# Scores of two tiles in one go, and a new order of loads, in a fused attention and feed-forward kernel

## The chip, the cores and the metric

The kernel runs on one core of one Trainium2 chip. The metric is device time in microseconds (us) from launch to end, as the median of several runs. Engines are named as in the profile: PE (TensorE, matrix products), DVE (VectorE), ACT (ScalarE), POOL (GpSimd) and SP (SyncE); PEld is PE's loading of weights.

## The reference, cut to what matters

Attention by chunks of 32 queries over 4 batches, 8 heads, 768 positions and head size 64, and then a gated feed-forward layer.

```
for c in range(24):                                   # chunks of 32 queries
    k_full = concat(mem_k, k[c*32-16 : c*32+32+8])     # 8 memory rows, 16 left, 32 own, 8 right
    scores = q_c @ k_full.T / 8
    a = exp(scores - max(scores)); a = a / sum(a)
    out[c] = a @ concat(mem_v, v[same rows])
x = out as [3072, 512]
y = (relu(x @ w_gate) * (x @ w_val)) @ w_out          # d_ff = 1536
```

Inputs are float32; the kernel casts on loading and computes in 16 bits with float32 sums.

## The kernel before, in words

A **tile** is 128 positions of one batch with all 8 heads: 24 tiles, a = 0 to 23, six per batch. Each goes through these steps, each an `op` of the plan (key in brackets):

- q and k are transposed (`t`) and copied into qT and kT (`tc`, `kc`). Tiles 0 to 5 come as pairs by `load_pair`; from tile 14 (q) or 15 (k) on the transposes are DMAs of SP's queue, before that PE products.
- `scores` (`s`, L289): 32 products of 64 rows x 32 columns of weights, moving 64 columns each, into the one buffer s_ps ([128, 2, 512] float32, pool `sps` with one buffer). A tile uses 256 of the 512 columns of each half.
- Row maximum (`max`), subtraction (`sub`), row sum (`sum`), reciprocal and normalisation (`nrm`) on DVE, the exponential (`exp`) on ACT. `sub` gives s_ps back.
- The probabilities are transposed (`p`, L348, by DMA from tile 14 on), copied (`pc`), multiplied with v_bd (`values`, `v`, L365), and the product is copied into xT (`x`).

v_bd holds v block by block with the memory rows: two sets, batch b in set b % 2. Set 0 is first filled with a pattern from mem_v (`pattern_load` on ACT's queue, cast, eight `spread` copies); then `load_v_rows` (L188) writes rows of v over it. The first chunk of the first batch has no left context, so `v_parts` gives it a small load of its own. Rows of batch b >= 2 can be loaded only when `values` of the last tile of batch b - 2 are done: the load of batch 2 depends on tile 5 and that of batch 3 on tile 11.

The **feed-forward part** works on blocks of tiles (`BLOCKS`, 3 or 4 tiles). `first` (`f`, L411) makes g_ps and v_ps for one of 12 slices m of d_ff; ACT does the relu, DVE the product (L423). `second` (`o`, L432) multiplies with w_out. Weights come in groups, w0 to w4 (slices 0-1, 2-3, 4-5, 6-8, 9-11). The two blocks of the first batch run their slices group by group in turn; the later blocks run one after the other. xT has two buffers, and a block gives its buffer back with its last `f`. Until the first block can start, PE is kept busy with `idle_product` (L403).

All loads with a cast are issued by POOL in the order of `LOADS`: Kr and Qr are pairs, `i` makes the identity matrix, vxy are v rows of batch 0 (half x, head pair y), w, o (w_out in halves), m (memory rows for later batches), z (zeroing of set 1), kN and qN single tiles, bxy v rows of batch x, head pair y (two loads each).

**The order of every engine's work** is worked out before by `schedule()`: it walks through time with a cost for each op, gives each engine the ready op of lowest priority value, and writes the ops down in that order. `LEAD` shifts the earliest start of later blocks' attention (`pace`), the priorities of the spreads and other small things. A load may be issued when fewer than 8 loads are in flight (`flying`); its data counts as there 1.5, 2.4 or 4.0 us after its turn on the queue ends. On the chip each engine follows the written order and waits by semaphores.

Of the kernel before, what the change touches and what calls it, by code (L numbers as in the profile page):

```python
# [10 lines left out]
F32 = mybir.dt.float32  # L11
# [10 lines left out]
def kernel(  # L22
# [27 lines left out]
    KW = CH + NMEM  # L50
    CTX = 16 + CH + 8
    NSET = 2
    BLOCKS = [3, 3, 3, 4, 3, 4, 4]
    LEAD = [22, -5, 16, 12, 4, 3, 14, 23, 5, -6, 7, 17, 24, 4, 24, 12, 12, 0, 3, -6, -3]
    LAST = ((0, 384), (384, 512))
    BY_DMA = (14, 15)
    BY_DMA_P = 14
    LANDING = 3.0
    PAIRS = 3
    SPLIT = 1  # L60
    EARLY = 2
    MEM_BY_SP = 0
    MEM_LEAD = (0,0,4,4)
    BY_DMA_X = 24
    BESIDE = 10.0
    LOADS = """K0 Q0 K1 i v01 Q1 Q2 K2 v00 v02 v03 w0 v12 w1 z1 v13 v11 w2 v10 w3
               m z3 w4 q7 q6 q8 z0 k8 k6 q9 k7 o1 k23 k9 o0 k13 z2 b13 b12 q13
               q21 k16 q12 b11 b10 k10 q17 k20 k11 q10 k18 q16 b21 q11 k15 q18 q14 k12 k14 b23
               b22 k21 k22 q15 b20 b30 q19 q20 q23 q22 b32 k17 b33 b31 k19"""

    KEY_RUNS = ((CH, KW, 0), (0, CH, NMEM), (KW, 64, KW))
    assert sum(BLOCKS) == NT and NMEM == 8 and D == 64 and H == 8
# [115 lines left out]
    def load_v_rows(b, par, hp, s0, s1, c0, c1):  # L188
# [2 lines left out]
            bass.AP(tensor=v.tensor, offset=v[b, 2 * hp + par, 0, 0].offset + (CH * c0 + s0 - 16) * D,  # L191
                    ap=[[D, s1 - s0], [CH * D, c1 - c0], [1, D]]))

    def v_parts(b, par, hp, c0, c1):
        parts = []
        if (b, par, hp, c0) == (0, 0, 0, 0):
            parts.append((b, par, hp, 16, CTX, 0, 1))
            c0 = 1
        if (b, par, hp, c1) == (B - 1, 1, HP - 1, NCH):
            c1 -= 1  # L200
            parts.append((b, par, hp, 0, 48, c1, c1 + 1))
        return parts + [(b, par, hp, 0, CTX, c0, c1)]
# [85 lines left out]

    def scores(a):  # L289
        b, t = divmod(a, TPB)  # L290
        s = sps.tile([128, 2, 512], F32, name="s_ps")
        keys = kT[b].rearrange("p h c s -> p h (c s)")
        for h2 in range(HP):
            for g in range(4):
                c = 4 * t + g
                lo, hi = max(KW * c - 16, 0), min(KW * c + 48, NCH * KW)
                o0 = 64 * h2 + lo - (KW * c - 16)
                for r in range(2):
                    d = slice(D * r, D * r + D)
                    nc.tensor.matmul(s[CH * g:CH * g + CH, r, o0:o0 + hi - lo],  # L300
                                     lhsT=qT[b][d, h2, CH * c:CH * c + CH],
                                     rhs=keys[d, h2, lo:hi], start=True, stop=True)
        S_ps[a] = s.rearrange("p a (h s) -> p a h s", s=64)[:, :, 0:HP, :]

    def row_max(a):
        t = a % TPB
# [154 lines left out]
    def psum(n):  # L461
# [3 lines left out]
    MARGIN = 1.2  # L465


    op("warm", {"DVE": 0.15}, lambda e: nc.vector.memset(warm, 0.0), prio=(-9,))
    op("warm2", {"ACT": 1.5}, lambda e: nc.scalar.activation(warm, warm, ACT.Exp), ["warm"], prio=(-9,), after=["vml"])  # L469
    op("vm00", {"DVE": 0.3}, lambda e: nc.vector.memset(vmem_0.rearrange("p h d -> p (h d)").bitcast(F32), 0.0),  # L470
       prio=(-8,), after=["im"])
    op("vml", {"ACT": 0.7}, lambda e: pattern_load(), prio=(-10,))
    op("kml", {"SP": 1.3}, lambda e: mem_load(), prio=(-8,))
    op("im", {"DVE": 0.12}, lambda e: nc.vector.memset(ident_h.bitcast(F32), 0.0), prio=(-8.5,), after=["warm"])
    op("ib", {"DVE": 0.25}, lambda e: nc.vector.tensor_copy(ident_b, ident_h), ["ident"], prio=(-7,))
# [45 lines left out]
    for a in range(NT):  # L521
        b, t = divmod(a, TPB)
        last = t == TPB - 1
        for i in (1, 0):
            if a < 2 * PAIRS:
                if a % 2:
                    continue
                ps = "fps" if a // 2 < EARLY else "aps"
                op(("t", a, i), {"PE": 0.64}, lambda e, a=a, i=i: pair_t(a // 2, i), [("qk2", a // 2, i), "ib", ("kv", b)],
                   (1, a - i, 0), [ps], ["pr"], pace(max(a - i, 0)))  # L530
                if i:
                    parts = k_parts(a // 2)
                    for n, (j, c0, c1) in enumerate(parts):
                        d = 0.07 + 0.0713 * (c1 - c0)
                        op(("kc", a // 2, n), {"ACT": d, "DVE": d},
                           lambda e, a=a, j=j, c0=c0, c1=c1: pair_k_copy(a // 2, j, c0, c1, engine[e]),
                           [("kc", a // 2, n - 1) if n else ("t", a, i)], (1, a - i + n // 2, n % 2), (),
                           [ps] * (n == len(parts) - 1))
                else:
                    for x in range(2):  # L540
                        op(("tc", a + x, i), {"ACT": 0.64, "DVE": 0.65}, lambda e, a=a, x=x: pair_q_copy(a // 2, x, engine[e]),
                           [("tc", a, i) if x else ("t", a, i)], (1, a + x, 0), (), [ps] * x)
            elif a < BY_DMA[i]:
                op(("t", a, i), {"PE": 0.23}, lambda e, a=a, i=i: qk_t(a, i), [("qk", a, i), "ib", ("kv", b)],
                   (1, a - i, 0), ["aps"], ["qk"], pace(max(a - i, 0)))
                op(("tc", a, i), psum(HP * 128), lambda e, a=a, i=i: qk_copy(a, i, engine[e]), [("t", a, i)],
                   (1, a - i, 0), (), ["aps"])
            else:
                op(("t", a, i), {"SP": 1.3}, lambda e, a=a, i=i: qk_dma(a, i), [("qk", a, i), ("kv", b)],
                   (1, a - i, 0), ["kt"] * i, ["qk"], [("p", a - i - 4)])  # L550
                if i:
                    op(("tc", a, i), {"ACT": 0.5}, lambda e, a=a, i=i: qk_copy(a, i, engine[e]),
                       [("t", a, i)], (1, a - i, 0), (), ["kt"], [("s", a - 2)] + pace(a - 1))
                else:
                    op(("tc", a, i), {"PE": 0.01}, lambda e: None, [("t", a, i)], (1, a - i, 0))
        op(("s", a), {"PE": 0.36}, lambda e, a=a: scores(a),
           [("tc", a, 0), keys_of(a), ("new", b) if b else ("new", 0, t // 3)] + ([] if last else [keys_of(a + 1, True)]),
           (1, a, 1), ["sps"],
           ["kv"] if last else [], ([("s", a - 1)] if a else []) + (pace(a) if a >= BY_DMA[0] else []) + behind(a))
# [14 lines left out]
        blk = block_of[a]  # L574
        j = a - starts[blk]
        ready = [("vl", b, 0 if b else t // 3, n) for n in range(2 * HP)]
        ready += [("mr", b, par, hp) for par in range(2) for hp in range(HP)] if b else []
        if a < BY_DMA_X:
            op(("v", a), {"PE": 0.41}, lambda e, a=a: values(a), [("pc", a)] + ready, (1, a, 10),
# [124 lines left out]
    def schedule():  # L704
# [30 lines left out]
        while len(started) < len(ops) + len(loads):  # L735
# [8 lines left out]
            while moved:  # L744
                moved = False
                for e in ("POOL", "PE", "ACT", "DVE", "SP"):
                    if free[e] > t + 1e-9:
                        continue
                    if e == "POOL":
# [97 lines left out]
```

## Time and profile before

| what | value |
|---|---|
| median of 3 runs | 239.06 us (238.92 to 239.76) |
| the profiled execution's own time | 238.81 us |
| its span, first to last instruction | 237.0 us |
| PE busy | 225.5 us (95%) |
| DVE busy | 150.9 us (64%) |
| ACT busy | 117.8 us (50%) |
| POOL busy | 91.5 us (39%) |
| granted TensorE clock | 1.000 |

The profile page tells busy time by engine, then by 40 slices of the span, then the chain of work that ended last, then groups of instructions. The timeline is a list of merged instructions with start and length. Products on PE overlap one another, so a group's length runs past the start of the next; what a group costs PE is read from start to start.

### The profile page before, as it was taken

Reading aid. Unit: us, or ns where it says so; the run is one execution under the profiler, and the core shown is the slowest. Engines: PE = TensorE matmul, PEld = TensorE weight load, DVE = VectorE, ACT = ScalarE, POOL = GpSimd, SP = SyncE. Lnnn points to the kernel's source line nnn. Section 1 sums busy time; section 2 is a strip of 40 time slices with the busy share of each in tenths; the row PEclk is TensorE's granted clock in tenths of the full one; section 3 lists DMA queues with packets and bytes.
Section 4 is the critical chain, followed back from the end, with each engine's and each line's share of the span. In section 5 each row is a group of like instructions: output and inputs, shape, how many; then the busy total and the mean of one; then the engine's idle time right before and its main releaser. Section 6 shows DMA issues by size and latency. Waiting matters only on the chain.

```text
span 237.0 us, 5892 instructions
## 1 busy us (share of the span) xinstructions
PE 225.5 (95%) x2432; PEld 125.6 (53%) x2432; DVE 150.9 (64%) x267; ACT 117.8 (50%) x251; POOL 91.5 (39%) x107
## 2 busy tenths in 40 slices
PE   0988989999999999999999999999999999999994
PEld 0777655665544666655444545664454444444442
DVE  5789953468999789954999146797775520234300
ACT  7988735444442786653643356655553331333212
POOL 6989998884875787059430000000000000000000
PEclk9999999999999999999999999999999999999999
DMA  7999999999999999979999344545420002200022
GB/s 75 163 160 179 161 180 179 165 192 172 151 174 211 199 179 133 118 127 149 141 150 117 75 149 111 69 46 121 127 48 0 0 4 88 88 0 0 3 88 89
DMA packets 121147, 27.17 MB, mean 115 GB/s; under 512 B 111264, under 2 KB 118176, under 8 KB 121120
## 3 DMA queue, kind: packets, MB, share of 16 engines
q0 software_dynamic: 101376, 16.61, 94.7%
q1 hardware_dynamic: 19664, 10.16, 18.5%
q8 instruction: 19, 0.31, 0.6%
q14 instruction: 8, 0.07, 0.1%
q10 hardware_dynamic: 80, 0.02, 0.0%
HBM read 33.24 MB, written 6.29 MB: 167 GB/s over the span
## 4 chain that ended last, share of the span: by engine, by line
PE 84%; POOL 8%; DMA 3%; ACT 2%; issue 1%; ACTq 0%; POOLq 0%
PE out_ps L432 26%; PE v_ps L411 25%; PE g_ps L411 25%; POOL v_bd L189 5%; PE xT_ps L365 4%; DMA v_bd<-in_v_dram 3%; PE s_ps L300 2%; PE qk_ps L266 2%; POOL w_gate_sb L121 1%; POOL w_val_sb L121 1%; POOL qk_p L220 1%; PE pT_ps L348 1%; ACT v_bd L94 1%; POOL v_bd L135 1%; ACT L469 1%
## 5 line engine op out<-in xcount | busy, mean ns | idle before, releaser
L423 DVE TENSOR_TENSOR gvT<-v_ps,g_relu 128x384 f16<-128x384 f32 (+1 forms) x84 | 51.2, 610 | 42.4 <-PE v_ps L411 42.0
L411 PE MATMUL v_ps<-xT,w_val_sb 128*128 128x384 f16 (+1 forms) x336 | 75.9, 349 | 0.3 <-DMA w_val_sb<-in_moe_w_val_dram 0.3
L411 PE MATMUL g_ps<-xT,w_gate_sb 128*128 128x384 f16 (+1 forms) x336 | 75.9, 349 | 0.0
L417 ACT ACTIVATE g_relu<-g_ps 128x384 f16<-128x384 f32 (+1 forms) x84 | 44.8, 534 | 57.9 <-PE g_ps L411 47.4
L432 PE MATMUL out_ps<-w_out_sb,gvT 128*128 128x512 f16 (+2 forms) x300 | 65.5, 370 | 0.0
L411 PEld LDWEIGHTS <-w_gate_sb 128*128 128x128 f16 x336 | 32.1, 98 | 28.1 <-DMA w_gate_sb<-in_moe_w_gate_dram 0.4
L411 PEld LDWEIGHTS <-w_val_sb 128*128 128x128 f16 x336 | 31.3, 98 | 26.8 <-DMA w_val_sb<-in_moe_w_val_dram 0.5
L189 POOL DMA_DIRECT2D v_bd<-in_v_dram x42 | 37.7, 910 | 16.6 <-PE xT_ps L365 9.3
L432 PEld LDWEIGHTS <-gvT 128*128 128x128 f16 x300 | 28.0, 98 | 30.0
L94 ACT COPY o_sb<-out_ps 128x512 f32<-128x512 f32 (+2 forms) x25 | 14.2, 569 | 32.8 <-PE out_ps L432 32.4
L164 DVE TENSOR_TENSOR v_bd<-vmem 8x768 int32<-8x768 int32 (+1 forms) x29 | 26.6, 944 | 1.1 <-ACT vmem L94 0.9
L327 ACT ACTIVATE p_exp<-dif 128x64 f16<-128x64 f32 (+2 forms) x72 | 19.6, 336 | 8.9 <-DVE dif L320 8.7
L313 DVE TENSOR_REDUCE mx<-s_ps 128x8 f32<-128x512 f32 x24 | 16.3, 677 | 5.5 <-PE s_ps L300 5.2
L331 DVE TENSOR_REDUCE sm<-p_exp 128x8 f32<-128x512 f16 x24 | 16.3, 678 | 5.2 <-ACT p_exp L327 5.1
L211 POOL DMA_DIRECT2D qk_b<-in_k_dram x18 | 16.0, 891 | 5.5 <-DMA w_out_sb<-in_moe_w_out_dram 2.8
L211 POOL DMA_DIRECT2D qk_b<-in_q_dram x18 | 16.0, 902 | 5.0 <-DMA v_bd<-in_v_dram 1.6
L342 DVE TENSOR_TENSOR p_n<-p_exp,rinv 128x512 f16<-128x512 f16 x24 | 16.4, 684 | 0.3
L320 DVE TENSOR_TENSOR dif<-s_ps,mx 128x512 f32<-128x512 f32 x24 | 16.4, 682 | 0.1
L365 PEld LDWEIGHTS <-v_bd 128*128 128x128 f16 x384 | 12.7, 96 | 5.2 <-issue 1.3
L365 PE MATMUL xT_ps<-pT,v_bd 128*128 128x32 f16 x384 | 13.0, 176 | 0.9 <-DMA v_bd<-in_v_dram 0.7
L94 ACT CAST xT<-xT_ps 128x512 f16<-128x512 f32 x17 | 9.9, 587 | 7.3 <-PE xT_ps L365 7.0
L403 PE MATMUL idle_ps<-ident_h 128*128 128x128 f16 x87 | 8.4, 238 | 4.8 <-POOL ident_h masks.py:199 4.8
(46 smaller groups left out, 125.5 us busy)
## 6 DMA issues: line engine op xcount, KB each, us to landing
out_dram<-o_sb SPq DMA_DIRECT2D x23, 256.0 KB, 2.1
v_bd<-in_v_dram POOLq DMA_DIRECT2D x23, 168.0 KB, 9.6
qk_b<-in_q_dram POOLq DMA_DIRECT2D x18, 128.0 KB, 9.3
qk_b<-in_k_dram POOLq DMA_DIRECT2D x18, 128.0 KB, 9.2
w_out_sb<-in_moe_w_out_dram POOLq DMA_DIRECT2D x2, 768.0 KB, 10.8
v_bd<-in_v_dram POOLq DMA_DIRECT2D x15, 84.0 KB, 4.9
qk_p<-in_k_dram POOLq DMA_DIRECT2D x3, 256.0 KB, 5.9
qk_p<-in_q_dram POOLq DMA_DIRECT2D x3, 256.0 KB, 5.3
```

Of the source, the lines that this page charges most:

```text
L94: nc.scalar.copy(o, i)
L164: nc.vector.tensor_tensor(out=o, in0=i, in1=i, op=ALU.bitwise_or)
L189: nc.gpsimd.dma_start(v_bd[b % NSET][64 * par + NMEM + s0:64 * par + NMEM + s1, hp, c0:c1, D * par:D * par + D], bass.AP(tensor=v.tensor, ...
L211: nc.gpsimd.dma_start(qk_b[a, i], bass.AP(tensor=x.tensor, offset=x[b, 0, 128 * t, 0].offset, ap=[[D, 128], [S * D, H], [1, D]]))
L320: nc.vector.tensor_tensor(out=SM[a, "dif"].rearrange("p h r s -> p r h s"), in0=S_ps.pop(a), in1=mx_b, op=ALU.subtract)
L327: nc.scalar.activation(p[:, :, :, s0:s0 + k1 - k0], dif[:, :, :, k0:k1], ACT.Exp, scale=SCALE)
L342: nc.vector.tensor_tensor(out=P_n[a], in0=SM.pop((a, "p")), in1=rinv_b, op=ALU.mult)
L365: nc.tensor.matmul(ps[:, hp, r], lhsT=v_bd[b % NSET][:, hp, 4 * t + g, :], rhs=x[:, hp, r], start=True, stop=True)
L411: nc.tensor.matmul(ps, lhsT=w[:, f, 128 * m:128 * m + 128], rhs=xTs[blk][:, f, :], start=(f == 0), stop=(f == NFC - 1))
L417: nc.scalar.activation(st["r", m], st.pop((0, m)), ACT.Relu)
L423: nc.vector.tensor_tensor(out=st["gv"][:, m, :], in0=st.pop((1, m)), in1=st.pop(("r", m)), op=ALU.mult)
L432: nc.tensor.matmul(st["o", t, cols], lhsT=st["gv"][:, m, 128 * t:128 * t + 128], rhs=w_out_sb[:, m, slice(*cols)], start=(m == 0), stop=(m ...
```

## The change

Four things: (1) from tile 6 on, the scores of tiles a and a+1 (a even) are one step of PE, side by side in the two 256-column parts of s_ps, and the buffer is given back after the second subtraction; (2) v rows of the first chunk are loaded by SP as float32 into vmem_f, behind a memset that clears 32 rows of it, and copied into v_bd by ACT or DVE; the pattern's load on ACT's queue now waits for that memset; (3) the plan counts a load as in flight until 0.2 us after its data is there, not until 1.0 us after its turn; (4) LOADS, LEAD and BLOCKS are new, so the blocks cut the tiles otherwise: 3, 3, 4, 4, 2, 4, 4.

```
-    BLOCKS = [3, 3, 3, 4, 3, 4, 4]
-    LEAD = [22, -5, 16, 12, 4, 3, 14, 23, 5, -6, 7, 17, 24, 4, 24, 12, 12, 0, 3, -6, -3]
+    BLOCKS = [3, 3, 4, 4, 2, 4, 4]
+    LEAD = [0, 1, 19, 16, 6, 23, 13, -1, -4, 7, 17, -5, 13, -6, 0, 6, 12, 4, -6, 3, -6]
+    TWO = 6
-    LOADS = """K0 Q0 K1 i v01 Q1 Q2 K2 v00 v02 v03 w0 v12 w1 z1 v13 v11 w2 v10 w3
-               m z3 w4 q7 q6 q8 z0 k8 k6 q9 k7 o1 k23 k9 o0 k13 z2 b13 b12 q13
-               q21 k16 q12 b11 b10 k10 q17 k20 k11 q10 k18 q16 b21 q11 k15 q18 q14 k12 k14 b23
-               b22 k21 k22 q15 b20 b30 q19 q20 q23 q22 b32 k17 b33 b31 k19"""
+    LOADS = """K0 Q0 i K1 Q1 v03 Q2 K2 v02 v00 v01 w0 v13 w1 w2 v10 v11 v12 w3 q7
+               q6 q10 k8 o0 z1 k7 k10 q9 m k6 w4 k9 q8 k13 o1 z0 b11 k11 z3 k21
+               k20 k12 z2 b12 b13 q21 b10 k15 q11 k18 q13 b22 k16 k23 k14 q15 b20 q14 q23 q22
+               q18 q12 b33 q16 q17 b21 b23 b31 k17 k19 k22 b30 q20 q19 b32"""
...
+    def load_first():
+        nc.sync.dma_start(vmem_f[NMEM + 16:64, 0, 0:D], ... v[0, 0, 0, 0] ... [[D, 64 - NMEM - 16], [1, D]])
...
     def v_parts(b, par, hp, c0, c1):
         if (b, par, hp, c0) == (0, 0, 0, 0):
-            parts.append((b, par, hp, 16, CTX, 0, 1))
             c0 = 1
...
     def scores(a):
-        s = sps.tile([128, 2, 512], F32, name="s_ps")
+        if a >= TWO and a % 2:
+            s = TMP.pop(("s", a - 1))
+        else:
+            s = TMP["s", a] = sps.tile([128, 2, 512], F32, name="s_ps")
+        h0 = HP * (a >= TWO and a % 2)
...
+    op("vf0", {"DVE": 0.1}, ... memset(vmem_f[0:32, 0, 0:D], 0.0), prio=(-10,))
+    op("vfl", {"SP": 0.4}, lambda e: load_first(), ["vf0"], prio=(-7.5,), after=["kml"])
+    op("vfc", {"ACT": 0.15, "DVE": 0.15}, ... copy(v_bd[0][0:64, 0, 0, 0:D], vmem_f[0:64, 0, 0:D]),
+       [("vfl", 3.2), ("vml", 1.2), ("spread", 0, 0)], prio=(1, 0, 9))
-    op("vml", {"ACT": 0.7}, lambda e: pattern_load(), prio=(-10,))
+    op("vml", {"ACT": 0.7}, lambda e: pattern_load(), ["vf0"], prio=(-10,))
...
-                       ... [("s", a - 2)] + pace(a - 1))     # k copy behind a DMA transpose
+                       ... [("s", a - 4)] + pace(a - 2))
...
+        if a >= TWO and a % 2:
+            op(("s", a), {"PE": 0.01}, lambda e: None, [("s", a - 1)], ...)
+        elif a >= TWO:
+            op(("s", a), {"PE": 0.60}, lambda e, a=a: (scores(a), scores(a + 1)), score_deps(a) + score_deps(a + 1),
+               (1, a, 1), ["sps"], (), after)
...
-           (1, a, 3), ["dif"], ["sps", "mx"])
+           (1, a, 3), ["dif"], ["mx"] if a >= TWO and a % 2 == 0 else ["sps", "mx"])
...
-                            flying.append(load_end)
                             done[key] = queue_end + (1.5 if n_load < 8 else 2.4 if n_load < 35 else 4.0)
+                            flying.append(done[key] + 0.2)
```

More of the change, by code (lines that the diff above doesn't have):

```diff
@@ L192, in load_v_rows @@
                     ap=[[D, s1 - s0], [CH * D, c1 - c0], [1, D]]))
+    def load_first():
+        nc.sync.dma_start(
+            vmem_f[NMEM + 16:64, 0, 0:D],
+            bass.AP(tensor=v.tensor, offset=v[0, 0, 0, 0].offset, ap=[[D, 64 - NMEM - 16], [1, D]]))
     def v_parts(b, par, hp, c0, c1):
@@ L296, in scores @@
                 lo, hi = max(KW * c - 16, 0), min(KW * c + 48, NCH * KW)
-                o0 = 64 * h2 + lo - (KW * c - 16)
+                o0 = 64 * (h0 + h2) + lo - (KW * c - 16)
                 for r in range(2):
@@ L302, in scores @@
                                      rhs=keys[d, h2, lo:hi], start=True, stop=True)
-        S_ps[a] = s.rearrange("p a (h s) -> p a h s", s=64)[:, :, 0:HP, :]
+        S_ps[a] = s.rearrange("p a (h s) -> p a h s", s=64)[:, :, h0:h0 + HP, :]
     def row_max(a):
@@ L465 @@
     MARGIN = 1.2
-    op("warm", {"DVE": 0.15}, lambda e: nc.vector.memset(warm, 0.0), prio=(-9,))
+    op("vf0", {"DVE": 0.1}, lambda e: nc.vector.memset(vmem_f[0:32, 0, 0:D], 0.0), prio=(-10,))
+    op("warm", {"DVE": 0.15}, lambda e: nc.vector.memset(warm, 0.0), prio=(-9,), after=["vf0"])
     op("warm2", {"ACT": 1.5}, lambda e: nc.scalar.activation(warm, warm, ACT.Exp), ["warm"], prio=(-9,), after=["vml"])
+    op("vfl", {"SP": 0.4}, lambda e: load_first(), ["vf0"], prio=(-7.5,), after=["kml"])
+    op("vfc", {"ACT": 0.15, "DVE": 0.15}, lambda e: copy(engine[e], v_bd[0][0:64, 0, 0, 0:D], vmem_f[0:64, 0, 0:D]),
+       [("vfl", 3.2), ("vml", 1.2), ("spread", 0, 0)], prio=(1, 0, 9))
     op("vm00", {"DVE": 0.3}, lambda e: nc.vector.memset(vmem_0.rearrange("p h d -> p (h d)").bitcast(F32), 0.0),
        prio=(-8,), after=["im"])
-    op("vml", {"ACT": 0.7}, lambda e: pattern_load(), prio=(-10,))
+    op("vml", {"ACT": 0.7}, lambda e: pattern_load(), ["vf0"], prio=(-10,))
     op("kml", {"SP": 1.3}, lambda e: mem_load(), prio=(-8,))
@@ L552, with score_deps @@
                     op(("tc", a, i), {"ACT": 0.5}, lambda e, a=a, i=i: qk_copy(a, i, engine[e]),
-                       [("t", a, i)], (1, a - i, 0), (), ["kt"], [("s", a - 2)] + pace(a - 1))
+                       [("t", a, i)], (1, a - i, 0), (), ["kt"], [("s", a - 4)] + pace(a - 2))
                 else:
                     op(("tc", a, i), {"PE": 0.01}, lambda e: None, [("t", a, i)], (1, a - i, 0))
[L556 to L559, printed above, removed]
+        def score_deps(a):
+            b, t = divmod(a, TPB)
+            return [("tc", a, 0), keys_of(a), ("new", b) if b else ("new", 0, t // 3)] + (
+                [keys_of(a + 1, True)] if t < TPB - 1 else [])
+        after = ([("s", a - 1)] if a else []) + (pace(a) if a >= BY_DMA[0] else []) + behind(a)
+        if a >= TWO and a % 2:
+            op(("s", a), {"PE": 0.01}, lambda e: None, [("s", a - 1)], (1, a, 1), (), ["kv"] if last else [])
+        elif a >= TWO:
+            op(("s", a), {"PE": 0.60}, lambda e, a=a: (scores(a), scores(a + 1)), score_deps(a) + score_deps(a + 1),
+               (1, a, 1), ["sps"], (), after)
+        else:
+            op(("s", a), {"PE": 0.36}, lambda e, a=a: scores(a), score_deps(a), (1, a, 1), ["sps"],
+               ["kv"] if last else [], after)
         op(("max", a), {"DVE": 0.61 + (0.2 if t == 0 or last else 0)}, lambda e, a=a: row_max(a), [("s", a)],
@@ L576 @@
         ready = [("vl", b, 0 if b else t // 3, n) for n in range(2 * HP)]
+        ready += ["vfc"] if a == 0 else []
         ready += [("mr", b, par, hp) for par in range(2) for hp in range(HP)] if b else []
```

## The prediction

> **What bounds the kernel.** I read the page from the top: busy time, the slices, the chain that ended last, the groups; then the waits of PE, the chain in order of time, and PE's timeline where it waits.
>
> ```profile
> PE 225.5 (95%) x2432; PEld 125.6 (53%) x2432; DVE 150.9 (64%) x267; ACT 117.8 (50%) x251; POOL 91.5 (39%) x107
> ...
> PE   0988989999999999999999999999999999999994
> DVE  5789953468999789954999146797775520234300
> ...
> PE 84%; POOL 8%; DMA 3%; ACT 2%; issue 1%; ACTq 0%; POOLq 0%
> ```
>
> PE is full from the fifth slice to the last. The first product of the feed-forward part starts at 24.23 us and the last ends at 233.99; what lies between costs time as PE work or as PE waiting. So three things can move the end: when that first product starts, how much PE time the work takes, and PE's waits. Before 34 us the chain goes over the loads:
>
> ```profile
> 26.54 0.75 POOL v_bd L189
> 27.30 6.14 DMA v_bd<-in_v_dram
> 33.57 0.98 PE xT_ps L365 x32
> ```
>
> The reader is to see that the last v rows of the first batch's second half land at 33.44 and that PE then goes on at once. PE's timeline around it, by starts:
>
> ```profile
> 29.22 0.81 PE L411 MATMUL v_ps<-xT,w_val_sb 128*128 128x384 f16 x4
> 30.06 0.82 PE L411 MATMUL g_ps<-xT,w_gate_sb 128*128 128x384 f16 x4
> 30.72 0.39 PE L348 MATMUL pT_ps<-ident_h,p_n 128*128 128x128 f16 x4
> 31.40 0.82 PE L411 MATMUL v_ps<-xT,w_val_sb 128*128 128x384 f16 x4 [0.29 <-DMA w_val_sb<-in_moe_w_val_dram]
> 32.06 0.81 PE L411 MATMUL g_ps<-xT,w_gate_sb 128*128 128x384 f16 x4
> 33.57 0.98 PE L365 MATMUL xT_ps<-pT,v_bd 128*128 128x32 f16 x32 [0.70 <-DMA v_bd<-in_v_dram]
> ```
>
> An undisturbed group of four takes 0.65 from start to start, a pT group 0.22. Here the steps are 0.84, 0.68 (for pT) and 1.51: 0.19 + 0.46 + 0.86 = 1.51 us of waiting for w2 and v. After 33.57 there is no such hole to the end.
>
> **Scores in pairs: the gain.** A score step in the full stretch:
>
> ```profile
> 53.43 0.81 PE L411 MATMUL v_ps<-xT,w_val_sb 128*128 128x384 f16 x4
> 54.08 0.81 PE L411 MATMUL g_ps<-xT,w_gate_sb 128*128 128x384 f16 x4
> 54.83 0.31 PE L300 MATMUL s_ps<-kT,qT 64*32 64x48 bf16 x32
> 55.07 0.82 PE L411 MATMUL v_ps<-xT,w_val_sb 128*128 128x384 f16 x4
> ```
>
> The group ahead takes 0.75 instead of 0.65: 0.10 for going in. From the first score product to the next group it is 0.24. One score product takes 0.19 (the page's mean is 194 ns) and the 32 run from first start to last end in 0.31, so their starts span 0.31 - 0.19 = 0.12 and the other 0.12 is for coming out. A lone step costs 0.10 + 0.12 + 0.12 = 0.34; a pair should cost 0.10 + 2 x 0.12 + 0.12 = 0.46, against 0.68. Saved: 0.22 a pair, for 9 pairs (tiles 6 to 23) **1.98 us**, all on PE's full stretch. No row shows two score steps in a row, so the bounds are 0 (the seam costs as much as before) and 9 x 0.24 = 2.2 (the second step nearly free); less than nothing is excluded, for the products are the same. I take 1.98, since inside a step no product shows a seam. [...]
>
> **What the pair holds.** s_ps comes back after four DVE steps (2 x 0.68 for maximum and 2 x 0.68 for subtraction, 2.7 us) instead of two. In the full stretch score steps are 3 to 8 us apart, and PE's only wait for this buffer is 0.4 at 15.5, before tile 6. So nothing is charged; if DVE were late, PE's queue would stand, feed-forward products and all, behind the scores.
>
> **Blocks.** Four-tile groups start every 0.865 us, three-tile ones every 0.65: 0.216 ns and 0.163 for one product, 0.42 ns a column both times. A two-tile product should take 0.109 us, longer than the 98 ns of its weight load. Seven blocks before and after: 0, bounds -0.5 and +1.0 (96 products whose weight loads might show).
>
> **The load by SP.** POOL loses one issue of 0.55 (the shortest of L189's); also z1, a POOL memset of 1.40, moves behind the first batch's rows. In exchange DVE gets a memset of 0.1 before everything, the pattern's load on ACT's queue waits for it (about 0.2 later, and with it casts and spreads), SP gets one issue behind kml's two, and ACT or DVE a small copy (0.26 on ACT by its small 128x128 copy, less on DVE) before the first values. DVE and ACT are 19.2 and 19.7 of the first 24 us busy, so I charge 0.2 + 0.15 = **+0.35** to the first product, bounds -1.5 and +1.0; below nothing because Q1 is issued some 2 us earlier and its tiles may come sooner.
>
> ```profile
> v_bd<-in_v_dram POOLq DMA_DIRECT2D x1, 5.0 KB, 6.1
> kmem_f<-in_mem_k_dram SPq DMA_DIRECT2D x2, 32.0 KB, 2.1
> ```
>
> The small load took 6.1 us to land through POOL and SP's took 2.1, but the first values need seven other loads that stay on POOL. [...]
>
> **The first 34 us.** Loads land at an even pace: by the sizes in the page's rows, w4 was the end of 6016 KB and landed at 42.25, the batch-1 rows the end of 10688 KB and landed by 73.8; counted from 3 us both are 152 KB/us. Up to the last row of the first batch the bytes are the same, so v lands at 33.3 again. But w2 now stands before v10, v11, v12 (about 340 KB, 2.2 us earlier), so the waits of 0.19 and 0.46 go and slices 4 and 5 of block 0 run through. From 24.23, twelve groups of 0.65 and three of 0.22 end at 32.7; what is late next is v again, 0.6 instead of 1.51. Gain **0.9**, bounds 0 and 1.5.
>
> **Sum.** 238.81 - 1.98 - 0.9 + 0.35 = 236.28 for an execution like the profiled one, which lay 0.25 under the median: **236.5**.
>
> **Rivals.**
>
> 1. *Loads that come later make PE wait.* w4 now stands behind eight single tiles and o0: 7808 KB, 54.4 by the pace, its gate half at 51.9. Slice 9 starts at 52.8 now, 0.9 sooner after, and needs the second half 0.65 later: up to 1.9 of waiting, unless PE has the transposes of tiles 6 to 9 (16 groups of 0.22) or pieces of the second product to do. The batch-1 rows are 256 KB later, 75.4 against values that start at 76.76, now for four tiles before block 2 instead of three: up to 1.5. For: the pace. Against: the plan knows both, and its order puts other work first. With 2.4 us it gives **238.9**.
>
> 2. *Batch 2's rows stand behind batch 3's* (slower). b33 must wait for the values of tile 11, and q16, q17, b21 and b23 wait behind it on POOL; the values of tiles 12 and 13, in block 3, need b21 and b23. The wait exists already:
>
> ```profile
> 103.42 1.94 POOL L189 DMA_DIRECT2D v_bd<-in_v_dram  x2 [9.34 <-PE xT_ps L365]
> ```
>
> Tile 11's values are at 102.64 there. From them to b23 issued are 0.5 + 2 x 0.97 + 2 x 0.89 + 4 x 0.98 = 8.1 us, to landing 9.6 more (the page's median), and 1.6 for values and copies: block 3 at 19.3 us after tile 11. It is due at about 114.9 (109.07 now, plus 7.8 for a wider block 2, plus 0.4 for tile 13, less 2.4 saved by then). So the point is tile 11 at 95.6: later, PE waits one for one. If tile 11 stays at 102.64 the wait is 7.0 and the time **243.5**. Against: tile 10's scores waited for k10, which now lands before w4, and tile 9 is done earlier; with q11 landing near 78, scores at 81 and 5.9 us of DVE steps at 60% of DVE (gates take the rest), tile 11 comes at about 93. For: DVE is busy 40.7 of the 44 us from 56 to 100, and the plan's 0.61 for a DVE step is 0.68 in the profile.
>
> 3. *The pair saves nothing*, because the seam stays or the held buffer gives the 2 us back: 236.5 + 2.0 = **238.5**.
>
> 4. *The start is faster too*: Q1 and the identity earlier bring the first product 1.5 us forward: **234.9**.
>
> **How the numbers follow.** Forecast 0.50 (235.2 to 237.8 by the bounds of seam, waits and start), rival 1 0.23 (237.6 to 239.8), rival 2 0.12 (from 239.8 up), rival 3 0.08, rival 4 0.07. A measurement of this kernel tells about 0.5% from no change, 1.2 us: 237.86 and 240.26. Faster: forecast, rival 4 and a fifth of rival 1, 0.62. Slower: rival 2 but for its mild end, 0.11. Same: the rest, 0.27. The range from 235.0 to 239.3 leaves out rival 2, half of rival 4 and the worst of rival 1.
>
> **What would show it.** Right: nine score steps of 64 products, each about 0.36 from first start to the next group; no hole in PE after 34 us; steps of 0.65 from 24 to 32. Wrong: a first product later than 25; holes on PE ahead of slice 9 (near 52), of block 2's first product (near 79) or of block 3's (near 115), with w_gate_sb, w_val_sb or v_bd named as what it waited for; two-tile products slower than 0.11.

## The result, and the profile after

The changed kernel takes 240.29 us in the median of 21 runs (239.35 to 243.6), the kernel before 238.89 in 21 runs beside it (238.15 to 240.04). The ratio is 1.006, with a 95% interval of 1.0039 to 1.008: slower, by a little more than what a measurement of this kernel can tell. Here and below, medians are over all runs, but ratios, and medians of the runs at full clock, leave out runs over 1.5% above the fastest of their kernel. The forecast was 236.5, the range 235.0 to 239.3. The profiled execution has an own time of 239.67 and a span of 237.9 at a mean granted clock of 0.999; before it was 238.81 and 237.0.

The page of the changed kernel, the lines that were shown of before (busy time, PE's slices, the engines on the chain that ended last):

```profile
PE 225.0 (95%) x2436; PEld 126.9 (53%) x2436; DVE 153.0 (64%) x270; ACT 117.0 (49%) x250; POOL 90.7 (38%) x106
...
PE   0986999999999999999999999999999999999994
...
DVE  5889974556899998496994699459963420234300
...
PE 91%; DVE 4%; DMA 2%; issue 1%; ACT 0%; ACTq 0%; POOLq 0%
```

POOL has left the chain (8% before), of DMA 2% stays (3% before), and PE's slices from the sixth to the ninth, which held an 8 before, are full. But the fourth is down from 8 to 6. PE's timeline there, first before, at the same score step:

```profile
21.33 0.34 PE L300 MATMUL s_ps<-kT,qT 64*32 64x64 bf16 x32
21.60 0.34 PE L403 MATMUL idle_ps<-ident_h 128*128 128x128 f16 x3
```

and after, there and then where the first batch's last rows are used:

```profile
20.53 0.55 PE L374 MATMUL xT_ps<-pT,v_bd 128*128 128x32 f16 x16
20.93 0.33 PE L412 MATMUL idle_ps<-ident_h 128*128 128x128 f16 x3
21.37 0.24 PE L309 MATMUL s_ps<-kT,qT 64*32 64x64 bf16 x13
23.26 0.27 PE L309 MATMUL s_ps<-kT,qT 64*32 64x64 bf16 x19 [1.64 <-issue]
...
25.87 0.82 PE L420 MATMUL g_ps<-xT,w_gate_sb 128*128 128x384 f16 x4
...
32.18 0.39 PE L357 MATMUL pT_ps<-ident_h,p_n 128*128 128x128 f16 x4
32.40 0.81 PE L420 MATMUL v_ps<-xT,w_val_sb 128*128 128x384 f16 x4
33.05 0.81 PE L420 MATMUL g_ps<-xT,w_gate_sb 128*128 128x384 f16 x4
33.70 0.95 PE L374 MATMUL xT_ps<-pT,v_bd 128*128 128x32 f16 x32
```

Two things are to be seen. From 25.87 to 33.70 no step carries a wait: the stalls of 1.51 us that the kernel before had there are gone. The first batch's last rows of v land at 31.67, before PE comes to them, where they landed at 33.44. And at 21.37 PE stops in the middle of one score step, after 13 of its 32 products, for 1.64 us, with "issue" as the reason: the profile shows nothing that PE waited for. The first product of the feed-forward part starts at 25.87 instead of 24.23, later by just the length of this stop.

**Where the 0.9 us of the profiled execution come from**, by PE's starts:

| stretch | before | after | difference |
|---|---|---|---|
| start to first feed-forward product | 24.23 | 25.87 | +1.64 |
| from there to the values of tile 3 (11 groups of four in both) | 9.34 | 7.83 | -1.51 |
| from there to the last product | 199.92 | 200.70 | +0.78 |

The new order of loads won all that PE waited for them, and the start lost it before. Of the last row, the scores account for 0.45 (below), and a second, small stop at 62.4 for 0.35 (a group of four that takes 1.00 from start to start instead of 0.65).

The median lies higher than the profiled execution, and this goes with the granted clock: in 11 of the 21 runs its mean is 0.997 or more (median 239.67), in the other 10 it is 0.992 or 0.993 (median 240.74). Of 123 runs of the kernel before that were made beside the experiments, 9 have one below 0.997. What such a run can look like is seen below, in the interleaved kernel.

### The profile page after: what moved, and what is told of

Its sections match the earlier page's. It is cut to its first block, busy times and chain, and to the rows that moved or that the text cites. A ratio compares the mean times of both kernels' runs of the same rounds, so it can differ in the third digit from the quotient of the medians.

```text
span 237.9 us, 5896 instructions
## 1 busy us (share of the span) xinstructions
PE 225.0 (95%) x2436; PEld 126.9 (53%) x2436; DVE 153.0 (64%) x270; ACT 117.0 (49%) x250; POOL 90.7 (38%) x106
## 4 chain that ended last, share of the span: by engine, by line
PE 91%; DVE 4%; DMA 2%; issue 1%; ACT 0%; ACTq 0%; POOLq 0%
PE v_ps L420 26%; PE g_ps L420 26%; PE out_ps L441 26%; PE xT_ps L374 4%; PE s_ps L309 3%; DMA qk_p<-in_k_dram 2%; PE qk_ps L271 2%; PE qk_ps L237 1%; PE pT_ps L357 1%; DVE mx L322 1%; DVE dif L329 1%; DVE sm L340 1%; PE idle_ps L412 1%; DVE kT L97 1%; DVE p_n L351 1%
## 5 line engine op out<-in xcount | busy, mean ns | idle before, releaser
L432 DVE TENSOR_TENSOR gvT<-v_ps,g_relu 128x512 f16<-128x512 f32 (+2 forms) x84 | 51.3, 613 | 54.3 <-PE v_ps L420 51.2
L420 PE MATMUL v_ps<-xT,w_val_sb 128*128 128x512 f16 (+2 forms) x336 | 75.9, 349 | 0.2 <-issue 0.2
L420 PE MATMUL g_ps<-xT,w_gate_sb 128*128 128x512 f16 (+2 forms) x336 | 75.8, 348 | 0.0
L426 ACT ACTIVATE g_relu<-g_ps 128x512 f16<-128x512 f32 (+2 forms) x84 | 45.0, 535 | 59.7 <-PE g_ps L420 50.6
L190 POOL DMA_DIRECT2D v_bd<-in_v_dram x41 | 37.1, 914 | 21.5 <-PE xT_ps L374 15.2
L95 ACT CAST xT<-xT_ps 128x512 f16<-128x512 f32 x16 | 9.1, 587 | 6.4 <-PE xT_ps L374 6.4
L237 PE MATMUL qk_ps<-ident_b,qk_p 128*64 128x128 bf16 x96 | 5.7, 283 | 6.5 <-DMA qk_p<-in_k_dram 6.0
## 6 DMA issues: line engine op xcount, KB each, us to landing
w_out_sb<-in_moe_w_out_dram POOLq DMA_DIRECT2D x2, 768.0 KB, 10.2
```

Of the source, the lines that this page charges most:

```text
L190: nc.gpsimd.dma_start(v_bd[b % NSET][64 * par + NMEM + s0:64 * par + NMEM + s1, hp, c0:c1, D * par:D * par + D], bass.AP(tensor=v.tensor, ...
L420: nc.tensor.matmul(ps, lhsT=w[:, f, 128 * m:128 * m + 128], rhs=xTs[blk][:, f, :], start=(f == 0), stop=(f == NFC - 1))
L426: nc.scalar.activation(st["r", m], st.pop((0, m)), ACT.Relu)
L432: nc.vector.tensor_tensor(out=st["gv"][:, m, :], in0=st.pop((1, m)), in1=st.pop(("r", m)), op=ALU.mult)
```

## The scores: what a pair costs

A pair in the changed kernel, in PE's timeline:

```profile
60.99 0.81 PE L420 MATMUL g_ps<-xT,w_gate_sb 128*128 128x384 f16 x4
61.74 0.68 PE L309 MATMUL s_ps<-kT,qT 64*32 64x64 bf16 x64
62.35 0.34 PE L420 MATMUL v_ps<-xT,w_val_sb 128*128 128x384 f16 x1
62.86 0.65 PE L420 MATMUL v_ps<-xT,w_val_sb 128*128 128x384 f16 x3 [0.18 <-issue]
```

From its first product to the next group a pair takes 0.61, where the forecast had 0.36. With 0.10 for going in that is 0.71, against 2 x (0.10 + 0.24) = 0.68 for two lone steps. By single starts, the first 32 products of each pair come every 3.9 ns, as in a lone step. Then there is a gap of 97 to 107 ns, and the other 32 come every 8.3 ns. Added up after 24 us, the starts of scores to the next group are 4.36 us for 18 lone steps and 5.67 for nine pairs: 1.31 more, less 9 x 0.095 for going in, 0.45 in all (two of the pairs hold a further stop of 0.06 and 0.14, ahead of their last product). The buffer that a pair holds longer costs nothing: behind 24 us no score step of the changed kernel waits for DVE.

**Lone steps in the changed kernel.**

```
-    TWO = 6
+    TWO = 100
```

> The changed kernel with every tile's scores as a step of its own again (the rest of the change stays). Theory A (a pair gains nothing: only the first 64 instructions of a score step, 32 weight loads and 32 products, come at 3.3 to 3.7 ns each; from then on an instruction takes about 4.2 ns after a gap of 0.10 us, so a pair costs 0.71 us with its way in against 0.68 for two steps): the time stays or falls, 239.4 to 240.2 against 240.3. Theory B (the prediction: a pair saves 0.22 and something else lost more): it rises by 9 x 0.22 = 2.0, to 242.2.

Measured: 240.38 us, ratio 1.0041 (1.0016 to 1.0067). In its profile, lone steps are again 0.24, and from first feed-forward product to last product it takes 207.94 us instead of 208.52. At full clock its runs have a median of 239.83 against 239.67 with pairs. The starts differ too (25.33 against 25.87), and the time is a little above the 239.4 to 240.2 that theory A had. So the pairs neither give nor take what can be told; the 1.98 is not there.

**Pairs alone, in the kernel before** (the code of the pair with LOADS, LEAD, BLOCKS and the rest of before).

> The kernel before with the pairs alone (loads, blocks, SP's load and flight count as before). Theory A: 238.9 plus 0.3 to 0.6 = 239.2 to 239.5, if the plan finds as good an order. Theory B: 236.9. A rival for what the pair costs, the buffer held for four DVE steps: holes on PE ahead of score steps, 0.5 or more each, named DVE.

Measured: 250.84, ratio 1.0495 (1.0467 to 1.0523). PE now stands up to 3.7 us, at 81, for single tiles of q and k: a pair asks for the loads of two tiles at once, and the old order brings the second too late. Behind this wait the granted clock is half for 10.2 us, and the mean of the run is 0.979. This prices the order and says nothing of the pair's own cost.

**The two tiles' products taken in turn**, so that no seam between tiles lies in the middle.

```
+        for h2 in range(HP):
+            for g in range(4):
+                scores_one(a, *x, h2, g)
+                scores_one(a + 1, *y, h2, g)
```

> The changed kernel with the 64 products of a pair in another order: the two tiles take turns, two products each. Theory A (the number of instructions counts): the gap of 0.10 us stays at the 33rd product and the second 32 stay at 8.3 ns each; time as the changed kernel, 240.0 to 240.6. Rival (the seam between tiles costs: a wait or the other columns of the buffer): the gap moves to the third product or goes, the slow rate spreads over all or goes, and the time moves by 9 x 0.1 or more.

Measured: 240.79, ratio 1.006 (1.0037 to 1.0083). The same pair as above:

```profile
62.60 0.71 PE L311 MATMUL s_ps<-kT,qT 64*32 64x64 bf16 x64
63.24 0.82 PE L434 MATMUL v_ps<-xT,w_val_sb 128*128 128x384 f16 x4
```

0.64 to the next group, and the gap (78 to 87 ns) again comes exactly at the 33rd product, in all nine pairs. (The new order isn't free: 4.5 ns a product ahead of the gap and 9.4 behind it, instead of 3.9 and 8.3.) So the place of the gap isn't set by the seam of two tiles or the other columns of the buffer, but goes with the count. 32 products are 64 instructions with their weight loads (the changed kernel's page counts 2436 of each). What sets that count no run shows.

## The start: PE runs out of instructions

The page lists a DMA queue of its own for instructions:

```profile
q8 instruction: 19, 0.31, 0.5%
```

Its transfers in the trace are of 16,384 bytes. A record is one instruction of PE's stream in the trace: products, weight loads and the few instructions for semaphores, counted together. PE's stops named "issue" come after records 449, 705, 961 or 1729, all multiples of 256 apart, in every kernel that has any (the small stop at 62.4 is the one at 1729): 16,384 / 256 = 64 bytes an instruction, an estimate from these two numbers. All 20 of these stops end 1.3 to 1.7 us after a transfer ended. So one transfer is a piece of 256 instructions, and PE stops at the end of a piece when the next isn't there. The transfers that bring the piece behind record 705 (the experiments, told below, by their edits; a stop counts where the reason is "issue"):

| kernel, times in us | PE at 449 | transfer starts | PE goes on behind 705 | longest stop at 705 | first feed-forward product |
|---|---|---|---|---|---|
| before | 16.45 | 18.95 | 21.40 | none | 24.23 |
| after | 16.66 | 20.76 | 23.26 | 1.6 | 25.87 |
| lone steps | 17.01 | 20.44 | 22.72 | 0.8 | 25.33 |
| weights further behind | 16.64 | 20.79 | 23.20 | 1.5 | 25.82 |
| z1 earlier | 17.16 | 20.79 | 23.14 | 1.1 | 26.75 |
| small load by POOL | 16.17 | 18.85 | 22.13 | none | 23.89 |
| lone, small load by POOL | 16.70 | 20.53 | 22.96 | none (0.6, put down to DVE) | 24.72 |
| before, small load by SP | 17.29 | 20.28 | 22.74 | none | 26.24 |
| before, memset only | 17.52 | 18.13 | 22.97 | none | 26.47 |

A transfer mostly takes 0.9 us and its piece is usable some 1.5 later: 20.76 + 0.89 = 21.65 and 23.26 after. PE reaches record 705 at 21.43 after and passes it at 21.40 before; what is late is the transfer, by 1.81. Before, PE passes 1.5 us after its transfer ended, so there too the piece comes with hardly any time to spare. In the kernel with lone steps and the small load by POOL, a wait of 0.6 that the profile puts down to DVE ends 1.5 us after the transfer as well; it may be one for instructions.

**More instructions.** If this is right, the kernel before must stop too when its idle product (L403), which only keeps PE busy, is cut into two halves of 64 columns: nearly the same time for the engine (nine whole ones take 0.67 us before, 18 halves 0.69 in this run), and 174 more instructions (87 products with their weight loads).

```
-        nc.tensor.matmul(TMP["idle"], lhsT=ident_h, rhs=ident_h, ...)
+        for c in range(0, 128, 64):
+            nc.tensor.matmul(TMP["idle"][:, c:c + 64], lhsT=ident_h, rhs=ident_h[:, c:c + 64], ...)
```

> The kernel before with every idle product cut in two of 64 columns: the same plan, 174 instructions more on PE before the first feed-forward product. Theory C: PE runs out of instructions in the fill, a hole of 0.5 to 2 us named issue appears before 25 us, the first feed-forward product comes 0.5 to 2 us later than 24.2, some runs show 0.993, and the time rises to 239.7 to 241. Rival (instructions always come in time): 239.2 within 0.3.

Measured: 242.48, ratio 1.01 (1.0051 to 1.0149). Its timeline:

```profile
23.70 0.50 PE L365 MATMUL xT_ps<-pT,v_bd 128*128 128x32 f16 x14 [0.39 <-ACT pT L94]
26.80 0.21 PE L365 MATMUL xT_ps<-pT,v_bd 128*128 128x32 f16 x2 [2.60 <-issue]
...
27.69 0.72 PE L412 MATMUL g_ps<-xT,w_gate_sb 128*128 128x384 f16 x2
```

PE stops inside one values step, after record 961, and the first feed-forward product is 3.5 us later than before. This stop, too, ends 1.45 us after a transfer ended. Nothing but the number of instructions was changed, so the stops go with PE's instruction supply. The loss is larger than the 239.7 to 241 that was expected; five of the six runs are at 0.993 or less of the clock, and the one at full clock took 240.17.

**Fewer instructions.** An idle product of 512 columns (the identity read four times), planned at 0.22 us:

> The changed kernel with idle products four times as long (512 columns) and a quarter as many, so PE's stream has some 100 instructions less before the first feed-forward product; nothing else is changed. Theory C (PE stands 1.64 us in the middle of a score step at 21.6 because its next 256 instructions have not come): the hole goes or moves, the first feed-forward product comes at 24.5 or sooner; the time falls by 0.1 to 0.8 to 239.5 to 240.2, since v rows landing at 33.3 hide most of it, and scatters less. Rival (that hole is what costs the 1.4 us): 238.9 or less. Rival (the hole is no instruction fetch): it stays where it is.

Measured: 240.71, ratio 1.0075 (1.0045 to 1.0104). No stop named "issue" is left, but the first feed-forward product is at 27.41, later than after: the idle products now fill 13.9 us of PE up to then (7.8 in the changed kernel), and real work stands behind them. Then products of 256 columns in every second slot, with the plan as it was, in three kernels: the changed one, the changed one with lone steps, and the kernel before.

```
+        TMP["slot"] = TMP.get("slot", 0) + 1
+        if TMP["slot"] % 2:
+            nc.tensor.matmul(TMP["idle"], lhsT=ident_h, rhs=<ident_h read twice>, ...)
```

> The changed kernel with idle products of 256 columns in every second of their slots: PE is as busy before the first feed-forward product, the order of all else is the same, and PE's stream has 90 instructions less (as many as were idle products). Theory C (the hole of 1.64 us at 21.6, in which PE has no instructions, is what the changed kernel loses: by itself, and through a window of 3.41 us at half clock right behind it in about half of the runs): no hole, first feed-forward product at 24.5 or sooner, mean clock 0.997 or more in all runs, time 238.3 to 239.0 against 240.3. Rival (v rows of the second half bound the next step, so the hole is free): 239.6 or more.

> The changed kernel with those idle products and with single score steps. Theory A and C together (a pair costs 0.05 to 0.1 more than two steps, and the hole is gone): 0.3 to 0.7 less than the same with pairs, 237.8 to 238.6, under the kernel before. Theory B (a pair saves 0.22): 2 us more than with pairs, 240.5 or so.

> The kernel before with those idle products. Theory C: it has no hole to lose, so 239.2 within 0.4, and the rare runs at 0.990 go. Rival (fewer instructions or longer idle products help as such): 238.3 or less.

Measured: 239.6 (ratio 0.9999, 0.9966 to 1.0031), 240.7 (0.9994, 0.9953 to 1.0035) and 238.94 (0.9967, 0.994 to 0.9995). At full clock the first two are 238.88 (9 runs) and 238.26 (6 runs, 237.91 to 240.68): again the pairs save nothing against lone steps, and both lie under the changed kernel's 239.67. But the first still stops 0.9 and 1.7 us for instructions, at records 449 and 705, against what theory C expected, and the kernel before gains 0.3% too. So fewer idle products help; that they help by taking these stops away is not shown.

**What a stop does to the clock.** The interleaved kernel's profile, in stretches of its span (busy times of PE, PEld, DVE, ACT and POOL, then the granted clock):

```profile
22.00:23.40 1.40, 0.32 (x21) 0.28 (x22) 1.02 (x2) 0.14 (x1) 1.35 (x3) 1.00 1.45 196
23.40:26.80 3.40, 3.40 (x73) 3.00 (x72) 2.01 (x4) 1.88 (x5) 2.28 (x4) 0.51 1.47 194
26.80:30.00 3.20, 3.20 (x23) 2.02 (x22) 3.13 (x7) 1.87 (x6) 2.02 (x3) 0.98 2.33 148
```

After a stop of 1.56 us at 21.5, PE is busy without a break at half the clock for 3.41 us (by the trace's record of the clock), and the mean clock of the run is 0.992. One such stretch in a span of 238 makes a mean clock of 0.993 (1 - 3.41 x 0.5 / 238), which is what about half of the changed kernel's runs show, and they take about 1.1 us more (240.74 against 239.67). The stop doesn't always bring it: the profiled executions of the changed kernel, of the weights further behind and of the first kernel with fewer idle products stop for 1.5 to 1.7 us and keep the full clock. The long idle products and the old order's start (below), which have no such stop, show no run of ten below 0.997; but the kernel before with fewer idle products, without a stop in its profile, has two of 12. So the half clock goes with these stops in four profiles; that they cause it is not shown.

## Why the pieces come late: what was tried

It remains why the transfer starts 4.1 us after PE has passed record 449 in the changed kernel, and 2.5 before.

**The old order's start**, with z1 where it was, and the rest of the new order:

> The changed kernel with the first 20 loads, to w3, in the order of the kernel before (z1 with them); the rest of its order, blocks, pairs and SP's load stay. Theory E: the fetch before the boundary at 21 to 22 us starts near 19 as in the kernel before, no hole over 0.5 us, first feed-forward product near 24.3, few runs at 0.993; the waits for w2 and v from 29 to 34 us come back; 239.2 to 239.8 against 240.3. Rival (the hole comes from something else of the change): a hole over 1 us and 240.3 or more.

Measured: 241.91, ratio 1.0124 (1.0101 to 1.0146), above what either theory had. No stop for instructions, the transfer at 19.84, 2.5 us after record 449, first product at 25.10, but v's rows are late again (values of tile 3 at 35.29), and the stretch behind takes 211.83.

**Weights further behind** ("w0 v13 v10 v11 w1 v12 w2 w3"), and **z1 back ahead of the rows** ("w0 z1 v13 w1 w2"):

> The changed kernel with v10 and v11 between w0 and w1 and v12 between w1 and w2, nothing else of the order changed. Theory E (w1 and w2 in a row delay the fetch of the next 256 instructions, which starts at 20.76 there and 4.1 us after PE crossed the boundary before): the fetch starts at 19.5 or sooner, the hole at 21.4 shrinks from 1.83 to under 0.8, and the time falls by 0.5 or more, to 239.7 or less. Rival (fetches are late whatever load stands in front): the hole stays over 1 us.

> The changed kernel with z1, POOL's memset of 1.4 us, put back among the first loads (between w0 and v13). Theory G (the fetch of PE's next 256 instructions starts late, at 20.76 against 18.95, because POOL runs ahead and more loads are in flight when it is due): the fetch starts at 19.6 or sooner, the hole at 21.4 falls from 1.83 to under 0.9, fewer runs at 0.993, time 239.0 to 239.8 against 240.3. Rival H (the start of the fetch does not hang on POOL's lead): fetch at 20.4 or later and a hole over 1.3, time 240 or more.

Measured: 242.14 (1.0133, 1.01 to 1.0166) and 240.72 (1.0061, 1.0028 to 1.0093). Both transfers start at 20.79, as in the changed kernel (20.76): neither weight groups in a row nor z1's absence among the first loads makes the transfer late.

**The small load back to POOL**, without the memset, SP's load and the copy:

> The changed kernel with the first chunk's rows loaded by POOL again, as in the kernel before (no load by SP, no memset ahead of the pattern, no copy). The prediction's term: the first feed-forward product 0.35 sooner. Theory G: POOL is 0.55 behind, so the fetch starts somewhat sooner and the hole shrinks by some 0.5; time 239.4 to 240.2. Rival H: hole as before, 240.0 to 240.4.

Measured: 241.2, ratio 1.0052 (1.0018 to 1.0085). The transfer starts at 18.85 and the start is 2.0 us earlier than in the changed kernel:

```profile
23.07 0.66 PE L413 MATMUL idle_ps<-ident_h 128*128 128x128 f16 x9
23.89 0.81 PE L421 MATMUL g_ps<-xT,w_gate_sb 128*128 128x384 f16 x4 [0.16 <-ACT xT L95]
```

But from there to the last product it takes 210.84 instead of 208.52: the plan comes out otherwise, and PE waits 0.7 at 35, 0.6 at 139 and elsewhere. So the time is no lower. It looked as if SP's load was the cause; three more kernels asked this: the same with lone steps, the kernel before with the small load by SP, and the kernel before with only the memset and the pattern's wait for it.

```
+    op("vf0", {"DVE": 0.1}, ... memset(vmem_f[0:32, 0, 0:D], 0.0), prio=(-10,))
-    op("vml", {"ACT": 0.7}, lambda e: pattern_load(), prio=(-10,))
+    op("vml", {"ACT": 0.7}, lambda e: pattern_load(), ["vf0"], prio=(-10,))
```

> The changed kernel with the scores of every tile as a step of their own and the first chunk's rows of v loaded by POOL again, as in the kernel before. Theory (PE's late start comes with the small load by SP, and the pairs save nothing): first product of the feed-forward part near 24, PE's third fetch of instructions near 18.9, no hole above 0.7 in the fill, and 237.5 to 238.7 us. Rival (the pairs do save 2 us and only the start costs): above 240.

> The kernel before, with one part of the change alone: the first chunk's rows of v by SP's queue, the memset ahead and the small copy. Theory (this load makes PE's third fetch of instructions late): the fetch starts near 20.8 instead of 18.95, a hole of 1 to 2 us follows near 21.5, the first product is at 25 to 26, and the time is 0.5 to 2 us longer. Rival (the fetch is late because of the order of the other loads): fetch near 19, no hole, first product near 24.2 and the time of the kernel before.

> The kernel before, with only the memset of 32 rows ahead of everything on DVE and the wait of the pattern's load for it; the small load stays with POOL. If the fetch is late because the pattern's load and its casts are late: fetch near 20.8 and a hole as in the changed kernel. If it goes with the load on SP's queue itself: fetch near 19, no hole, and within 0.3 us of the kernel before.

Measured: 241.57 (1.0095, 1.0072 to 1.0117), 239.91 (1.0021, 1.0008 to 1.0035) and 241.07 (1.0082, 1.0047 to 1.0116). The theory falls, as do the expectations of all three: with the small load on POOL the transfer starts as late as 20.53, and the memset alone gives the earliest one, 18.13. The second has its transfer late (20.28) as expected, but no stop. The two costs don't add up to the whole loss either: 237.5 to 238.7 was expected of the first, where PE also waits 1.0 and 1.1 at 135 and 137 for ACT and DVE. What sets the start of these transfers stays open. The second, with its start at 26.24, shows also that 2 us of start need not cost 2 us of time: by the ratio it is 0.5 us above the kernel before, and by the profiled executions 1.26. The values of tile 3 wait for their rows anyway and start at 33.29, with 9 groups of four done instead of 11.

The third kernel shows something else. The memset alone makes the start 2.24 us later, with no stop for instructions. In its timelines of ACT, POOL and PE:

```profile
3.87 4.22 ACT L94 COPY v_bd<-vmem 128x1536 f16<-128x1536 f16 x3
```

```profile
5.63 1.60 POOL L189 DMA_DIRECT2D v_bd<-in_v_dram  x2 [0.66 <-ACT v_bd L94]
...
17.12 0.78 POOL L121 DMA_DIRECT2D w_gate_sb<-in_moe_w_gate_dram  x1 [1.91 <-DMA qk_p<-in_k_dram]
```

```profile
26.47 0.81 PE L411 MATMUL g_ps<-xT,w_gate_sb 128*128 128x384 f16 x4
...
35.40 0.78 PE L365 MATMUL xT_ps<-pT,v_bd 128*128 128x32 f16 x24 [2.47 <-DMA v_bd<-in_v_dram]
```

Before, these stand at 3.62, 5.39, 15.08, 24.23 and 33.57. The 0.25 of the memset passes on to POOL as 0.24; then POOL, under a plan worked out anew, waits 1.91 for a load of k, and what stands behind it is about 2 us late. This is not what delays the changed kernel's start: there POOL issues this first weight load at 14.13, sooner than before.

## The other parts of the order

**w2 earlier in the kernel before**, alone and with the idle products in every second slot ("w0 v12 w1 w2 v13 v11 v10 w3 / m z1 z3"):

> The kernel before with one step of the new load order: w2 right behind w1, then v13, v11, v10 and w3, and z1 behind m. Theory D (the prediction's step: early w2 takes away PE's waits of 0.19 and 0.46 and leaves 0.6 of 0.86): values of tiles 3 and 4 at 33.6 as before or 0.3 sooner, but one or two feed-forward groups more before them, time 0.6 to 0.9 less than before. Theory E (two weight groups in a row hold up the next load of PE's instructions, so PE stands at the 256-instruction boundary near 21.9): a hole of 0.5 to 2 us there, time as before or up to 1 us more.

> The same with the idle products of 256 columns in every second slot. Theory D with the 0.3% that these idle products gave the kernel before: 1.0 to 1.6 less than the kernel before. Theory E: a hole at one of the boundaries again, within 0.5 of the kernel before.

Measured: 239.89 (1.0034, 1.0016 to 1.0053) and 239.43 (1.0031, 1.0 to 1.0062). The values of tile 3 start 0.5 and 0.8 us earlier with one group more done, so the waits were real and can go. No stop for instructions came at 21.9, so theory E fails, and theory D's 0.6 to 0.9 us at the end isn't there either. The stretch behind loses it again: from first feed-forward product to last, 210.19 and 209.83 against 209.26.

**Lone steps with z1 earlier**, in the changed kernel:

> The changed kernel with z1 early and single score steps. Theories A and G: 0.2 to 0.6 less than with pairs and z1 early, 238.6 to 239.4, at or under the kernel before. Theory B (pairs save): 2 us more than with pairs. Rival H: 240 or more, by the hole.

Measured: 238.39, ratio 0.9965 (0.9945 to 0.9985): beside the kernel before with fewer idle products (0.9967), the only version whose interval lies below 1, by 0.2 to 0.6%. All but one of its 13 runs have the full clock. The same order with pairs took 240.72; there PE waits 1.3 us for DVE at 82.7, which the lone steps' plan doesn't have. The one profile of this kernel is of the remaining run, of 242.26 us at a clock of 0.991, with a stop of 3.1 us for instructions at 16.7. From its first feed-forward product to its last product, all at full clock, it takes 207.88 us, against 210.34 with pairs and 208.52 in the changed kernel; what the start of the faster runs looks like isn't shown.

## Why the prediction was wrong

- **The pair (-1.98): the step that failed.** "Inside a step no product shows a seam" was true of 32 products and was carried on to 64. The second 32 cost 0.10 + 0.26 instead of 0.12. Going in (0.10) and coming out (0.12) were right, and the saving of one of each is eaten: 0.71 against 0.68. The lower bound of 0 ("the products are the same") was passed too, by 0.45 in all. The third rival had this outcome, at 2.0 us and with a chance of 0.08, but by other ways: a seam that stays or the held buffer, neither of which the runs show.
- **The first product (+0.35): came out as +1.64.** The mechanism was another one than priced: not ACT's late pattern but PE's instruction supply, which no step of the prediction had. This is the second step that failed. A first product later than 25 was named as the sign of failure. The upper bound of 1.0 was made from DVE, ACT and POOL only; PE was taken as ready for whatever came.
- **The waits of the first 34 us (-0.9): right in kind, and short.** All 1.51 are gone. w2 came in time, as forecast, but "v lands at 33.3 again" was wrong: POOL issued the last rows at 25.66 instead of 27.30, and they landed at 31.67, so even a start at 24.23 would have met them (24.23 + 7.83 = 32.06). That is no gain at the end, since the late start ate it: both kernels are at 11 groups when tile 3's values start, at 33.57 and 33.70.
- **Blocks (0): right.** Groups of four two-tile products take 0.44, 0.109 a product, as worked out (the 0.216 and 0.163 of the prediction are us, not ns).
- **Late loads (rival 1) and the rows of batch 2 (rival 2): neither came.** There is no wait near 52, 79 or 115. At block 3, in PE's timeline:

```profile
115.75 0.95 PE L374 MATMUL xT_ps<-pT,v_bd 128*128 128x32 f16 x32
116.55 2.10 PE L441 MATMUL out_ps<-w_out_sb,gvT 128*128 128x512 f16 x9
118.49 1.03 PE L420 MATMUL g_ps<-xT,w_gate_sb 128*128 128x512 f16 x4
```

The values of tile 11 were done by 98.7, and the second products cover what is left.

The sum, corrected: 236.28 + 1.98 + 0.45 (pairs) + 1.29 (start) - 0.61 (waits) + 0.33 (behind 34 us, the stop at 62.4) - 0.05 (tail) = 239.67, the profiled execution. What the median has above it goes with the lower clock of ten of the 21 runs.

## What to carry to other kernels

A saving per step may be carried on to a longer step only as far as a row shows it; where a burst gets longer than any in the trace, bound it by the whole of what a second burst costs now. Where an engine with many short instructions stands in "issue" in the middle of a step, count its instructions from the start: products that only keep it busy use up its supply (here 174 instructions more came with a stop of 2.6 us). And in a kernel whose order a planner works out, undoing one part gives a new order all over, so compare stretches between milestones, not only times.

## What the runs showed of the hardware

- PE's instructions come by transfers of 16,384 bytes (256 instructions), usable some 1.5 us after a transfer of 0.9; between records 449 and 705 PE uses a piece up in 3.2 us (more idle products, 16.20 to 19.41) to 5.0 (the kernel before, 16.45 to 21.40), and where the next isn't there it stands for up to 2.6 (more idle products) or 3.1 (lone steps with z1 earlier).
- The transfer of the piece behind record 705 starts 0.6 (memset only) to 4.4 us (interleaved) after PE has passed record 449; what sets this wasn't found.
- Products of 64 rows and 32 columns start every 3.9 ns for the first 32; behind them there is a gap of 0.08 to 0.11 us, and then one every 8.3 ns (4.5 and 9.4 where two tiles take turns).
- A stop of PE of 1.1 us (z1 earlier), 1.56 (interleaved), 2.6 (more idle products) or 3.1 us (lone steps with z1 earlier) was followed by 3.41 us at half the granted clock; stops of 1.5 to 1.7 us in three other profiles were not.
